# Re-cutting the transfers of a long-convolution and soft-MoE kernel to multiples of 16 rows

## The chip, the cores and the metric

The kernel runs on one core of a Trainium2 chip. The metric is device time in microseconds, taken as the median over several runs. A separate profiled execution gives the busy times, waits and transfers; its span is a little shorter than the timed runs, because it goes from the first to the last instruction.

## The reference

The input `x` is 8 sequences of 5696 tokens with 128 channels; `h` is one filter of 5696 taps for each channel. Each sequence is convolved with the filter along the tokens (a causal convolution, computed over a doubled length in the frequency domain). The 45568 result rows then go through a soft mixture of experts:

```python
Yf = rfft(x, n=2*S) * rfft(h, n=2*S);  y = irfft(Yf)[:, :S]      # 8 x 5696 x 128
logits = y.reshape(N, D) @ phi                                   # N = 45568, 32 slots
d = softmax(logits, over tokens);   slot_input = d.T @ y
slot_out[e] = relu(slot_input[e] @ w1[e]) @ w2[e]                # 8 experts x 4 slots
out = softmax(logits, over slots) @ slot_out
```

All data are float32.

## The kernel before

**Tiling.** The 5696 tokens of a sequence are laid out as 89 rows (`R1`) of 64 (`N2`). The transform is split into one over the rows (90 frequencies, `N1`, of which two halves of 45, `NP`) and one over the 64 columns. Everything is written as matrix products with constant tables: `s1` (rows to frequencies), `wt` and `vt` (columns, forward and back), and `i1` (frequencies back to rows).

**Stages.** The filter is group 0, the sequences are groups 1 to 8. A group is worked in 8 chunks of 4 columns and their mirror columns.

- Stage A: `load_x` (L190) brings a chunk of x or h into one of three `xc` tiles, as 80 rows at partition `X0` = 20 and 9 rows behind them. `fold` (POOL, L201) adds or subtracts the mirrored columns over all 128 partitions. `stage_a` multiplies by `s1` (PE, L212, two products per half), ACT copies the result from PSUM into `fst` (L214), and SyncE stores two blocks of 45 rows, from partitions `F0` = 6 and `F1` = 82, into the DRAM tensor `fd` (L218, f<-fst).
- Stage B: `load_g` (L236) brings 4 frequencies of `fd` back as a `gt` tile of 128 partitions, PE multiplies by `wt` (L250), DVE multiplies by the filter's spectrum (L268, L277), PE multiplies by `vt` (L292), ACT copies (L297), and SyncE stores the result into the DRAM tensor `zd` (L300, z<-zst).
- Stage C works on pairs of chunks, 32 in all: `load_pair` (L328, zc<-z) brings 90 rows of `zd`, 16 KB each, as 64 rows at partition 32 and 26 rows at partition 0. `stage_c1` multiplies by `i1` (L347) over all 128 partitions and builds the convolved rows `y`. The following stages transpose `y` (L375), form the logits (L384), the two softmaxes, and the weighted sum of rows per slot (`dispatch`, L460), one for each pair.
- At the end the experts are computed, and the output is formed and stored (L817, L828).

**Order.** Stages A, B and C of different groups are interleaved by a plan written out by hand: each step `t` does one chunk of A, one or two units of B, and half a pair of C. All large transfers are issued by SyncE in program order. Transfers take turns on eight completion counters, so a transfer waits for the one that stands eight places before it, besides the waits for its data.

**The edges of the blocks.** The products of L212 and L347 run over all 128 partitions, but x fills 89 of them and z 90. The rest must hold zeros: the `xc` tiles (L177) and the `zc` tile (L314) are cleared at the start. For the last pairs a second z tile, `zd`, is placed in memory that the front's tables have given up. There the rows from 26 to 31, between the two blocks, are copied from `zc` (L657), and L347 uses 96 partitions on that tile (`used`).

Of the kernel before, what the change touches and what calls it, by code (L numbers as in the profile page):

```python
# [10 lines left out]
F32 = mybir.dt.float32  # L11
# [5 lines left out]

def z_blocks(n):

    return [(0, 64, 32), (64, n - 64, 0)]  # L20


def transform_tables(S, N1, N2, CH, X0, F0, F1):

    N, R1, HALF, P = N1 * N2, S // N2, N2 // 2, 2 * N2
    k1 = np.arange(N1)
    alpha = np.pi * (k1 + 0.5) / N1
    m1 = np.arange(R1) - (N1 - 1) / 2
    a1 = np.outer(m1, alpha)  # L40
    s1 = np.stack([np.cos(a1), -np.sin(a1), -np.cos(a1)], 1)
    a0 = np.outer(alpha, np.arange(N1 // 2) + 0.5)
    i1 = np.stack([np.cos(a0), -np.sin(a0), -np.cos(a0)], 1)
    NP = N1 // 2
    part = s1
    s1 = np.zeros((P, 3, P))
    for a, p in enumerate((F0, F1)):
        s1[X0:X0 + R1, :, p:p + NP] = part[:, :, a * NP:(a + 1) * NP]
    part = i1[np.arange(N1).reshape(2, NP).T.reshape(-1)]
    i1 = np.zeros((P, 3, N2))  # L50
    for r, n, p in z_blocks(N1):
        i1[p:p + n, :, 0:NP] = part[r:r + n]
    k2 = np.arange(N2)
    omega = np.pi * (k1[:, None] + 2 * N1 * k2[None] + 0.5) / N
    m2 = np.arange(HALF) - (N2 - 1) / 2
    a2 = m2[None, :, None] * omega[:, None, :]
    w = np.concatenate([np.cos(a2), np.sin(a2)], 1)
    back = np.arange(N2).reshape(2, HALF // CH, CH).transpose(1, 0, 2).reshape(-1)
    NU = (NP + 1) // 2
    turn = (N1 - 1) / 2 * alpha[:, None] + (N2 - 1) / 2 * omega  # L60
    wq = np.zeros((2, N2, NP, N2))
    vq = np.zeros((2, N2, NU, 2, N2))
    tn = np.zeros((2, N2, 2, (NU + 1) // 2, 2, 2))
    for a in range(2):
        wq[a] = w[a * NP:(a + 1) * NP].transpose(1, 0, 2)
        for q in range(NP):
            vq[q % 2, :, q // 2, a] = w[a * NP + q][back].T
            tn[q % 2, :, 0, q // 4, a, q // 2 % 2] = np.cos(turn[a * NP + q]) / N
            tn[q % 2, :, 1, q // 4, a, q // 2 % 2] = np.sin(turn[a * NP + q]) / N
    wq, vq, tn = [t.reshape(P, *t.shape[2:]) for t in (wq, vq, tn)]  # L70
    return [np.ascontiguousarray(t, dtype=np.float32) for t in (s1, i1, wq, vq, tn)]
# [3 lines left out]
def kernel(  # L75
# [24 lines left out]
    nc = tc.nc  # L100
    P = 128
    B, S, D = x.shape
    NSL = moe_phi.shape[1]
    E, _, F = moe_w1.shape
    SPE = NSL // E
    NFC = F // P
    N1, N2 = 90, 64
    R1, HALF, NP = S // N2, N2 // 2, N1 // 2
    CH = 4
# [6 lines left out]
    HP = P // 2  # L116
    NQ = NJ // 2
    assert S == R1 * N2 and R1 == N1 - 1 and D == P and CH == Q == 4
    SPLIT = R1 // 16 * 16
    X0, F0, F1 = 20, 6, 82  # L120
    ctx.enter_context(tc.manual_schedule())

    t_s1, t_i1, t_w, t_v, t_turn = [
        nc.inline_tensor(t, f"tab_{n}").ap()
        for n, t in zip(("s1", "i1", "w", "v", "turn"), transform_tables(S, N1, N2, CH, X0, F0, F1))]
    fd = [nc.dram_tensor(f"f_{g}", (2, N2, NP, 2, D), F32, kind="Internal").ap() for g in range(B + 1)]
    zd = [nc.dram_tensor(f"z_{b}", (NP, 2 * N2, 2, D), F32, kind="Internal").ap() for b in range(B)]
    cd = nc.dram_tensor("c_t", (P, B * NQ, Q, 2, MH), F32, kind="Internal").ap()

# [6 lines left out]
    i1 = const.tile([P, 3, HP], F32, name="i1")  # L136
# [24 lines left out]
    s1 = apool.tile([P, 3, P], F32, name="s1", tag="s1", bufs=1)  # L161
    wt = fconst.tile([P, NP, HP], F32, name="wt")
    vt = fconst.tile([P, NU, 2, HP], F32, name="vt")
    turn = fconst.tile([P, 2, NW, 2, 2], F32, name="turn")
# [8 lines left out]
    xs = {}  # L173
    xf = [apool.tile([P, CH, D], F32, name=f"x{i}", tag=f"x{i}", bufs=1) for i in range(2)]
    xcs = [apool.tile([P, 2, CH, D], F32, name=f"xc{i}", tag=f"xc{i}", bufs=1) for i in range(3)]
    for t_ in xcs:
        nc.vector.memset(t_[:, :, :, :], 0.0)  # L177

    def load_x(c):
        if c >= (B + 1) * NJ:  # L180
            return
        g, j = divmod(c, NJ)
        src = (h if g == 0 else x[g - 1]).rearrange("(a n) d -> a n d", n=N2)
        t_ = xcs[c % len(xcs)]
        gap = N2 - CH * (2 * j + 1)
        for r in (slice(0, SPLIT), slice(SPLIT, R1)):
            v = src[r, CH * j:CH * (j + 1), :]
            v = bass.AP(tensor=v.tensor, offset=v.offset,
                        ap=[v.ap[0], [gap * D, 2], [1, CH * D]])
            nc.sync.dma_start(  # L190
                out=t_[X0 + r.start:X0 + r.stop, :, :, :].rearrange("p s n d -> p s (n d)"), in_=v)
        xs[c] = t_

    folded = {}
# [1 line left out]
    def fold(c, comp):  # L196
        if c not in xs:
            return
        t_ = xs.pop(c) if comp else xs[c]
        y_ = xf[comp]  # L200
        nc.gpsimd.tensor_tensor(out=y_[:, :, :], in0=t_[:, 0, :, :], in1=t_[:, 1, ::-1, :],  # L201
                                op=AL.subtract if comp else AL.add)
        folded[(c, comp)] = y_

    def stage_a(c, comp):
        g, j = divmod(c, NJ)
        src = folded.pop((c, comp))
        tab = (0, 1) if comp == 0 else (1, 2)
        st = apool.tile([P, CH, 2, D], F32, name="fst", tag="fst", bufs=5)
        for G in range(2):  # L210
            p = bank()
            nc.tensor.matmul(p[:, :], s1[:, tab[G], :],  # L212
                             src[:, :, :].rearrange("p n d -> p (n d)"), start=True, stop=True)
            nc.scalar.activation(st[:, :, G, :],  # L214
                                 p[:, :].rearrange("p (n d) -> p n d", d=D), AF.Copy)
        n0 = comp * HALF + CH * j
        for a, p in enumerate((F0, F1)):
            nc.sync.dma_start(  # L218
                out=fd[g][a, n0:n0 + CH, :, :, :].rearrange("n q c d -> q n (c d)"),
                in_=st[p:p + NP, :, :, :].rearrange("k n c d -> k n (c d)"))  # L220


    gs, prods = {}, {}
# [80 lines left out]


    zs, ys, Ls, ds = {}, {}, {}, {}
    zn = used = None
    ybufs = [ypool.tile([P, Q * CH, D + 1], F32, name=f"y{i}") for i in range(2)]
    zring = [ypool.tile([P, 2, 2, CH, 2, D], F32, name="zc")]
    lt = ypool.tile([P, CH, 2, HP], F32, name="lt")  # L310
    dt = ypool.tile([P, CH, 2, HP], F32, name="dt")
    om, op = [ypool.tile([P, CH, D], F32, name=n) for n in ("om", "op")]
    yt = ypool.tile([D, Q * CH, 2, MH], F32, name="yt")
    nc.vector.memset(zring[0][:, :, :, :, :, :], 0.0)  # L314
    for t_ in (lt, dt):
        nc.vector.memset(t_[:, :, :, :], 0.0)
    for t_ in ybufs:
# [15 lines left out]

    def stage_c1(T, between):
        t_ = zs.pop(T)
        kr = used if t_ is zn else P
        y_ = ybufs.pop(0)
        ybufs.append(y_)

        def part(v, f):  # L340
            k = (2 * v + f) * CH
            return y_[:, k:k + CH, 0:D] if f == 0 else y_[:, k + CH - 1:k - 1:-1, 0:D]

        def product(o, tab, q):
            p = bank()
            for h_ in range(2):
                nc.tensor.matmul(p[h_ * HP:(h_ + 1) * HP, :], i1[0:kr, tab, :],  # L347
                                 t_[0:kr, h_, o, :, q, :], start=True, stop=True)
            return p[:, :].rearrange("p (n d) -> p n d", d=D)

        def fold_out(even, minus, plus):
            nc.vector.tensor_tensor(out=plus, in0=even, in1=minus, op=AL.add)  # L352
            nc.vector.tensor_tensor(out=minus, in0=even, in1=minus, op=AL.subtract)

        b_, a_ = product(0, 1, 1), product(0, 0, 0)
        nc.scalar.activation(part(0, 0), b_, AF.Copy)
        fold_out(a_, part(0, 0), part(1, 0))
        between()
        b_, a_ = product(1, 1, 0), product(1, 2, 1)
        nc.scalar.activation(om[:, :, :], b_, AF.Copy)  # L360

        def after():
            fold_out(a_, om[:, :, :], op[:, :, :])
            for v, o_, eng in ((1, op, nc.gpsimd), (0, om, nc.vector if tail else nc.gpsimd)):
                for part_, sign in ((part(v, 1), AL.subtract), (part(v, 0), AL.add)):
                    eng.tensor_tensor(out=part_, in0=part(v, 0), in1=o_[:, :, :], op=sign)  # L366

        ys[T] = y_
        return after
# [191 lines left out]
    for t in range(last_front + 1):  # L561
# [82 lines left out]
        if NA < t <= NA + E:  # L644
# [2 lines left out]


    T = V + 1
    (_, n0, p0), (_, n1, p1) = z_blocks(N1)  # L650
    gap, used = slice(p1 + n1, p0), p0 + n0
    front.close()
    rings.append(mid.enter_context(tc.tile_pool(name="ps2", bufs=4, space=PSUM)))
    last = work.enter_context(tc.tile_pool(name="last", bufs=1))
    tail["last"] = last
    zn = last.tile([P, 2, 2, CH, 2, D], F32, name="zd")
    nc.sync.dma_start(out=zn[gap, :, :, :, :, :].rearrange("k h o n c d -> k (h o n c d)"),  # L657
                      in_=zring[0][gap, :, :, :, :, :].rearrange("k h o n c d -> k (h o n c d)"))
    zring.insert(0, zn)
    load_pair(V + 2)  # L660
    nc.sync.dma_start(out=w1s[:, E - 1, :], in_=moe_w1[E - 1])
# [4 lines left out]
    y_ = tail["pool"].tile([P, Q * CH, D + 1], F32, name="y2", tag="y2", bufs=1)  # L666
# [6 lines left out]
    for q in range(Q):  # L673
        r = slice(q * NSL, (q + 1) * NSL)
# [19 lines left out]
    for V in range(T, NT):  # L694
# [30 lines left out]
        else:  # L725
            for i in range(4 * (V - T - 1), min(4 * (V - T), E), 2):
                nc.sync.dma_start(
                    out=w2s[:, i:i + 2, :, :],
# [7 lines left out]
    p = bank()  # L736
# [127 lines left out]
```

## Time and profile before

| | before |
|---|---|
| time, median of 3 runs | 924.22 us (922.99 to 924.59) |
| span of the profiled execution | 914.5 us |
| granted TensorE clock, mean | 0.945 |
| bytes moved by transfers | 272.43 MB |
| L212 matmuls (stage A) | 576, 611 ns on average |
| L347 matmuls (stage C) | 512 |
| f<-fst stores | 288 of 180 KB |
| x and h loads | 72 of 320 KB and 72 of 36 KB |
| z loads | 32 of 1024 KB and 32 of 416 KB |

An engine's busy share is an average over stages with different limits. Three stretches matter here: the start, in which only stages A and then B run (to about 180 us), the middle in which all three stages run side by side (180 to 686 us), and the end. In a table of stretches each row gives its length, the busy time of each engine with the number of instructions, the granted clock, the mean busy share of the 16 DMA engines, and the rate of their traffic. The chain of waits runs back from the last instruction: a piece named DMA is time in which the work that ended last stood waiting for that transfer to land.

### The profile page before, as it was taken

The page shows a single profiled execution, that of the slowest core. Times are in us where ns is not written, and L with a number is a line of the kernel's source. Part 1 is how long each engine was busy: PE and PEld are TensorE (multiplying, and loading weights), DVE is VectorE, ACT ScalarE, POOL GpSimd, SP SyncE. Part 2 cuts the span into 40 slices and gives each one's busy share as a digit, 9 for nine tenths or more (in the row PEclk, how much of TensorE's full clock was granted, in tenths as well). Part 3 has the DMA queues.
Part 4 walks back from the last instruction along what each step waited for, and adds up shares of the span by engine and source line. Part 5 has one row for each costly group of instructions (what it writes and reads, how often), then busy time and mean ns, then how long its engine had stood idle before and what let it go on. Part 6 is the DMA issues. An engine that isn't in the chain of part 4 may idle for free.

```text
span 914.5 us, 19226 instructions
## 1 busy us (share of the span) xinstructions
PE 812.2 (89%) x7220; PEld 425.9 (47%) x7220; DVE 645.8 (71%) x928; ACT 481.1 (53%) x888; POOL 405.2 (44%) x385
## 2 busy tenths in 40 slices
PE   6968888799999999999999999999988776978893
PEld 2323344344454444544555445444444443345783
DVE  3058767667888878877888777868888885774552
ACT  4624445456556565655666565555654344474442
POOL 4624333245555555555555555555533432472000
PEclk9989999999999999999999999999999998788865
DMA  9999899999999999999999999989989998751798
GB/s 302 269 282 310 256 326 347 292 323 340 285 324 331 304 281 323 320 329 280 329 323 317 289 317 313 311 281 325 334 266 338 305 295 206 223 220 74 281 404 340
DMA packets 156550, 272.43 MB, mean 298 GB/s; under 512 B 11766, under 2 KB 114422, under 8 KB 153317
## 3 DMA queue, kind: packets, MB, share of 16 engines
q1 hardware_dynamic: 155883, 270.85, 91.7%
q8 instruction: 58, 0.95, 0.4%
q10 hardware_dynamic: 576, 0.36, 0.2%
q14 instruction: 33, 0.27, 0.1%
HBM read 142.86 MB, written 128.21 MB: 296 GB/s over the span
## 4 chain that ended last, share of the span: by engine, by line
PE 61%; DMA 27%; issue 4%; ACT 2%; DVE 2%; POOL 2%; SPq 1%; DVEq 0%; POOLq 0%; ACTq 0%
PE bank L212 19%; PE bank L347 10%; PE bt L250 9%; DMA zc<-z 8%; PE bz L292 7%; DMA gt<-f 6%; DMA out_dram<-o 4%; PE bank L375 3%; PE bank L460 3%; DMA zd<-z 3%; DMA z<-zst 2%; DMA f<-fst 2%; PE bank L384 2%; PE bank L436 2%; PE op L817 1%
## 5 line engine op out<-in xcount | busy, mean ns | idle before, releaser
L201 POOL TENSOR_TENSOR x<-xc 128x512 f32<-128x512 f32 x144 | 183.1, 1273 | 260.5 <-PE bank L212 156.9
L212 PE MATMUL bank<-x,s 128*128 128x512 f32 x576 | 273.9, 611 | 9.7 <-POOL x L201 9.6
L214 ACT ACTIVATE fst<-bank 128x512 f32<-128x512 f32 x288 | 171.8, 597 | 94.7 <-PE bank L212 88.3
L297 ACT ACTIVATE zst<-bz 128x1024 f32<-128x1024 f32 x96 | 93.2, 971 | 195.2 <-PE bz L292 191.5
L268 DVE TENSOR_TENSOR p<-bt,Hi 128x1024 f32<-128x1024 f32 x96 | 113.0, 1177 | 107.3 <-PE bt L250 107.1
L212 PEld LDWEIGHTS bank<-x,s 128*128 128x128 f32 x576 | 102.1, 192 | 126.9 <-issue 94.1
L250 PE MATMUL bt<-gt,wt 64*64 64x256 f32 x1620 | 117.4, 397 | 40.0 <-DMA gt<-f 19.8
L347 PE MATMUL bank<-zc,i 128*64 128x512 f32 x480 | 118.0, 614 | 8.5 <-DMA zc<-z 6.2
L277 DVE TENSOR_TENSOR yf<-bt,p 128x512 f32<-128x512 f32 x192 | 119.4, 663 | 3.3
L268 DVE TENSOR_TENSOR bt<-bt,Hr 128x1024 f32<-128x1024 f32 x96 | 113.0, 1178 | 0.0
L250 PEld LDWEIGHTS bt<-gt,wt 64*64 64x64 f32 x1620 | 55.9, 134 | 117.0 <-issue 61.7
L292 PE MATMUL bz<-yf,vt 64*64 64x256 f32 x1440 | 103.7, 386 | 0.0
L366 POOL TENSOR_TENSOR y<-y,op 128x512 f32<-128x512 f32 x64 | 77.4, 1209 | 11.8 <-DVE op L352 9.1
L292 PEld LDWEIGHTS bz<-yf,vt 64*64 64x64 f32 x1440 | 61.8, 136 | 21.1
L366 POOL TENSOR_TENSOR y<-y,om 128x512 f32<-128x512 f32 x54 | 64.0, 1185 | 2.1
L347 PEld LDWEIGHTS bank<-zc,i 128*64 128x64 f32 x480 | 30.9, 138 | 70.3 <-issue 47.4
L375 PE MATMUL bank<-ident,y 109*128 109x109 f32 x512 | 57.5, 268 | 0.7 <-DVE y L366 0.7
L375 PEld LDWEIGHTS bank<-ident,y 109*128 109x128 f32 x512 | 51.2, 146 | 12.9 <-POOL L L449 6.2
L421 POOL MEMSET dt<- 64x8 f32 x32 | 3.4, 106 | 115.9 <-issue 69.2
L377 ACT ACTIVATE yt<-bank 128x360 f32<-128x360 f32 x128 | 50.2, 483 | 2.1 <-PE bank L375 2.1
L817 PE MATMUL op<-so,cT 32*128 32x128 f32 x704 | 46.2, 369 | 4.3 <-ACT o L826 3.4
L268 DVE TENSOR_TENSOR p<-bt,turn 128x1024 f32<-128x1024 f32 (+1 forms) x12 | 14.1, 1176 | 50.7 <-PE bt L250 50.6
(97 smaller groups left out, 861.5 us busy)
## 6 DMA issues: line engine op xcount, KB each, us to landing
f<-fst SPq DMA_DIRECT2D x288, 180.0 KB
gt<-f SPq DMA_DIRECT2D x99, 512.0 KB
z<-zst SPq DMA_DIRECT2D x88, 512.0 KB
zc<-z SPq DMA_DIRECT2D x30, 1024.0 KB
xc<-in_x_dram SPq DMA_DIRECT2D x64, 320.0 KB
out_dram<-o SPq DMA_DIRECT2D x16, 1024.0 KB
zc<-z SPq DMA_DIRECT2D x30, 416.0 KB
out_dram<-o SPq DMA_DIRECT2D x8, 768.0 KB
```

The lines of the kernel that those rows point to most:

```text
L201: nc.gpsimd.tensor_tensor(out=y_[:, :, :], in0=t_[:, 0, :, :], in1=t_[:, 1, ::-1, :], op=AL.subtract if comp else AL.add)
L212: nc.tensor.matmul(p[:, :], s1[:, tab[G], :], src[:, :, :].rearrange("p n d -> p (n d)"), start=True, stop=True)
L214: nc.scalar.activation(st[:, :, G, :], p[:, :].rearrange("p (n d) -> p n d", d=D), AF.Copy)
L250: nc.tensor.matmul(bt[q * HP:(q + 1) * HP, a, o, :], wt[r, 2 * i + q, :], t_[r, 2 * o + q, :, :].rearrange("p c d -> p (c d)"), start=True ...
L268: nc.vector.tensor_tensor(out=p_, in0=pv, in1=h_, op=AL.mult)
L277: eng.tensor_tensor(out=y_[r, 0:k, c, :], in0=pv[:, :, c, :], in1=pi[r, 0:k, 1 - c, :], op=op_)
L292: nc.tensor.matmul(bz[a * HP:(a + 1) * HP, q, o, :], vt[r, i, a, :], y_[r, a * m + o, :, :].rearrange("p c d -> p (c d)"), start=True, sto ...
L297: nc.scalar.activation(st[:, 0:m, 0:n, :].rearrange("p o q x -> p q o x"), bz[:, 0:n, 0:m, :], AF.Copy)
L347: nc.tensor.matmul(p[h_ * HP:(h_ + 1) * HP, :], i1[0:kr, tab, :], t_[0:kr, h_, o, :, q, :], start=True, stop=True)
L366: eng.tensor_tensor(out=part_, in0=part(v, 0), in1=o_[:, :, :], op=sign)
L375: nc.tensor.transpose(p[:, i * TR:(i + 1) * TR], ys[T][0:TR, k * CH + i, 0:D], ident[0:TR, 0:TR])
L817: nc.tensor.matmul(pq[q][:, k * D:(k + 1) * D], cT[rows, b, r0:r0 + RW, :] if k < n else cL[rows, :, :], so4[rows, :], start=True, stop=True)
```

## The change

Each transfer that had another number of rows is cut into pieces of 16, 32, 48 or 64 rows.

- f: `fd` gets 48 frequencies for each half instead of 45 (`QR`); the three added rows are zero columns of `s1`. The stores take 48 partitions from `F0` = 8 and `F1` = 72.
- z: the second piece is 32 rows from row 58, six of which the first piece has already brought. In `i1` the repeated rows are zero. The two pieces fill partitions 0 to 95 without a gap.
- x: three pieces in place of two: 64 rows at partition 32, 16 rows at the even partitions 0 to 30, and 16 rows, seven of them repeated, at the odd partitions 1 to 31. In `s1` the repeated rows are zero.
- The fold and the products L212 and L347 run over 96 partitions (`KR`), all of which are now filled. So the clearing of `xc` and `zc`, the copy of the gap into `zd`, and `used` go.

The purpose is that every transfer has row counts that divide evenly over the 16 DMA engines, and that no cleared partitions are needed.

```diff
 def z_blocks(n):
-    return [(0, 64, 32), (64, n - 64, 0)]
+    return [(0, 64, 32), (n - 32, 32, 0)]
+def x_blocks(n):
+    return [(0, 64, 32, 1), (64, 16, 0, 2), (n - 16, 16, 1, 2)]
...
-    SPLIT = R1 // 16 * 16
-    X0, F0, F1 = 20, 6, 82
+    F0, F1 = 8, 72
+    QR = 48
+    KR = 96
...
-    fd = [nc.dram_tensor(f"f_{g}", (2, N2, NP, 2, D), F32, kind="Internal").ap() for g in range(B + 1)]
+    fd = [nc.dram_tensor(f"f_{g}", (2, N2, QR, 2, D), F32, kind="Internal").ap() for g in range(B + 1)]
...
-    for t_ in xcs:
-        nc.vector.memset(t_[:, :, :, :], 0.0)
...
-        for r in (slice(0, SPLIT), slice(SPLIT, R1)):
-            v = src[r, CH * j:CH * (j + 1), :]
+        for r, n, p, step in x_blocks(R1):
+            v = src[r:r + n, CH * j:CH * (j + 1), :]
...
-                out=t_[X0 + r.start:X0 + r.stop, :, :, :].rearrange("p s n d -> p s (n d)"), in_=v)
+                out=t_[p:p + (n - 1) * step + 1:step, :, :, :].rearrange("p s n d -> p s (n d)"), in_=v)
...
-        nc.gpsimd.tensor_tensor(out=y_[:, :, :], in0=t_[:, 0, :, :], in1=t_[:, 1, ::-1, :],
+        nc.gpsimd.tensor_tensor(out=y_[0:KR, :, :], in0=t_[0:KR, 0, :, :], in1=t_[0:KR, 1, ::-1, :],
...
-            nc.tensor.matmul(p[:, :], s1[:, tab[G], :],
-                             src[:, :, :].rearrange("p n d -> p (n d)"), start=True, stop=True)
+            nc.tensor.matmul(p[:, :], s1[0:KR, tab[G], :],
+                             src[0:KR, :, :].rearrange("p n d -> p (n d)"), start=True, stop=True)
...
-                in_=st[p:p + NP, :, :, :].rearrange("k n c d -> k n (c d)"))
+                in_=st[p:p + QR, :, :, :].rearrange("k n c d -> k n (c d)"))
...
-    nc.vector.memset(zring[0][:, :, :, :, :, :], 0.0)
...
-                nc.tensor.matmul(p[h_ * HP:(h_ + 1) * HP, :], i1[0:kr, tab, :],
-                                 t_[0:kr, h_, o, :, q, :], start=True, stop=True)
+                nc.tensor.matmul(p[h_ * HP:(h_ + 1) * HP, :], i1[0:KR, tab, :],
+                                 t_[0:KR, h_, o, :, q, :], start=True, stop=True)
...
-    nc.sync.dma_start(out=zn[gap, :, :, :, :, :].rearrange("k h o n c d -> k (h o n c d)"),
-                      in_=zring[0][gap, :, :, :, :, :].rearrange("k h o n c d -> k (h o n c d)"))
```

More of the change, by code (lines that the diff above doesn't have):

```diff
@@ L18, in z_blocks, with transform_tables @@
 def z_blocks(n):
-    return [(0, 64, 32), (64, n - 64, 0)]
-def transform_tables(S, N1, N2, CH, X0, F0, F1):
+    return [(0, 64, 32), (n - 32, 32, 0)]
+def x_blocks(n):
+    return [(0, 64, 32, 1), (64, 16, 0, 2), (n - 16, 16, 1, 2)]
+def transform_tables(S, N1, N2, CH, F0, F1):
     N, R1, HALF, P = N1 * N2, S // N2, N2 // 2, 2 * N2
@@ L47, in transform_tables @@
     for a, p in enumerate((F0, F1)):
-        s1[X0:X0 + R1, :, p:p + NP] = part[:, :, a * NP:(a + 1) * NP]
+        done = 0
+        for r, n, p0, step in x_blocks(R1):
+            for i in range(n):
+                if r + i >= done:
+                    s1[p0 + i * step, :, p:p + NP] = part[r + i, :, a * NP:(a + 1) * NP]
+            done = max(done, r + n)
     part = i1[np.arange(N1).reshape(2, NP).T.reshape(-1)]
     i1 = np.zeros((P, 3, N2))
+    done = 0
     for r, n, p in z_blocks(N1):
-        i1[p:p + n, :, 0:NP] = part[r:r + n]
+        i1[p + done - r if r < done else p:p + n, :, 0:NP] = part[max(r, done):r + n]
+        done = r + n
     k2 = np.arange(N2)
@@ L124 @@
         nc.inline_tensor(t, f"tab_{n}").ap()
-        for n, t in zip(("s1", "i1", "w", "v", "turn"), transform_tables(S, N1, N2, CH, X0, F0, F1))]
-    fd = [nc.dram_tensor(f"f_{g}", (2, N2, NP, 2, D), F32, kind="Internal").ap() for g in range(B + 1)]
+        for n, t in zip(("s1", "i1", "w", "v", "turn"), transform_tables(S, N1, N2, CH, F0, F1))]
+    fd = [nc.dram_tensor(f"f_{g}", (2, N2, QR, 2, D), F32, kind="Internal").ap() for g in range(B + 1)]
     zd = [nc.dram_tensor(f"z_{b}", (NP, 2 * N2, 2, D), F32, kind="Internal").ap() for b in range(B)]
@@ L306 @@
     zs, ys, Ls, ds = {}, {}, {}, {}
-    zn = used = None
+    zn = None
     ybufs = [ypool.tile([P, Q * CH, D + 1], F32, name=f"y{i}") for i in range(2)]
@@ L335, in stage_c1 @@
         t_ = zs.pop(T)
-        kr = used if t_ is zn else P
         y_ = ybufs.pop(0)
@@ L649 @@
     T = V + 1
-    (_, n0, p0), (_, n1, p1) = z_blocks(N1)
-    gap, used = slice(p1 + n1, p0), p0 + n0
     front.close()
```

## The prediction

> **What bounds the kernel now.** I read the page first (busy shares, packet counts, chain of waits), then the stretch table, then the chain in order of time, then the matmul groups with shapes kept apart.
>
> ```profile
> PE 812.2 (89%) x7220; PEld 425.9 (47%) x7220; DVE 645.8 (71%) x928; ACT 481.1 (53%) x888; POOL 405.2 (44%) x385
> DMA packets 156550, 272.43 MB, mean 298 GB/s; under 512 B 11766, under 2 KB 114422, under 8 KB 153317
> q1 hardware_dynamic: 155883, 270.85, 91.7%
> PE 61%; DMA 27%; issue 4%; ACT 2%; DVE 2%; POOL 2%; SPq 1%; DVEq 0%; POOLq 0%; ACTq 0%
> ...
> xc<-in_x_dram SPq DMA_DIRECT2D x64, 320.0 KB
> ...
> zc<-z SPq DMA_DIRECT2D x30, 416.0 KB
> ```
>
> TensorE holds most of the chain, but transfers hold 27% of it; the last two lines are two of the transfers that the change re-cuts (320 KB are 80 rows, 416 KB are 26). The stretch table (length, then busy time of PE, PEld, DVE, ACT, POOL, granted clock, DMA share, GB/s) splits that up:
>
> ```profile
> 46.00:114.00 68.00, 53.49 (x304) 22.38 (x304) 48.58 (x56) 23.68 (x40) 24.38 (x20) 0.92 0.92 283
> 180.00:686.00 506.00, 491.81 (x4352) 246.50 (x4354) 400.26 (x575) 297.90 (x543) 267.74 (x249) 1.00 0.98 311
> 760.00:835.00 75.00, 56.84 (x455) 30.69 (x455) 47.09 (x83) 42.27 (x100) 38.60 (x46) 0.81 0.68 206
> ```
>
> In the long middle, PE is busy 97% and the 16 DMA engines 98%: both are nearly full. From 46 to 114 us PE is idle for 14.5 us with the DMA at 92%. The chain shows where the middle loses time:
>
> ```profile
> 213.89 1.02 PE bank L460 x32
> ...
> 235.13 1.03 PE bank L460 x32
> ...
> 298.23 12.96 DMA zc<-z
> 311.33 1.94 PE bank L347 x8
> ...
> 651.30 1.02 PE bank L460 x32
> ```
>
> A pair of steps (one L460 to the next) takes 20.7 to 21.2 us where PE flows; from 213.89 to 651.30 there are 20 pairs, so 21.87 us on average. The difference, about 0.7 us a pair, is a handful of stalls on zc<-z and gt<-f loads that stand deep in a full queue.
>
> [...] the counter writes are f 4320, gt 1728, z 1536, zc 928, x 1800 and 1198 for the rest, 64 for the four ACT-issued constants, and 256 short rows of phi and turn: 11766 in all, as the page has. [...] from 180 to 686 us the 2 KB packets of x took 127 ns on average against a floor of 82, the 16 KB packets of z 835 against 611 [...], while 88% of the 128-partition gt packets are near their floor. [...] 94% of the 1 KB packets sit at 46 ns[...]. [...] here the 64 KB pitch of z still gives 611 ns per 16 KB, so a pitch of 48 KB for f instead of 45 KB is costed at nothing.
>
> **The change part by part.** *Engines per transfer.* [...] Worth by itself: 0. [...]
>
> *Where the x rows land.* [...] That is the ratio of the z load [...], whose mean is 1.37 of its floor, against 1.55 for x now. I take 115 ns a packet: 12 packets x 12 ns = 0.14 us a load [...]. Bounds: 127 ns (nothing) and 82 ns (0.54 us). There are 38 such loads in the middle: 5.5 us (0 to 20, but PE, busy 492 of 506, caps it near 12). Some ten more from 46 to 114 us: 1.5 us. These are on the path as far as the engines' queue sets the pair's time.
>
> *SyncE's queue.* 72 more x issues at 0.4 to 0.5 us (median 394 ns for h, 520 for x): 36 us of SP time, 2 per pair. Behind them stand the f stores and the gt load of the same step. SP is idle some 7 us in a pair, waiting on engines, so I cost it at 0 to 1 us in all while the queue is full. The eight completion counters are handed out in turn, so each transfer waits for the one eight places before. In before, gt mostly waits for the 64-row z load; in after for the 32-row one, which lands a little later, and the fourth f store waits for the 64-row one. Behind gt is the z store, and PE L250 waits for gt (27.5 us in all). The queue ahead of gt holds the same transfers either way, and 3 to 5 us of work is still in flight: I take +1.5 us in total, bounds 0 and +10.
>
> *96 partitions.* The trace has the same matmul on 96 rows, in the last pairs (before, too, skips the zero rows there):
>
> ```profile
> L347 PE MATMUL bank<-zc,i x480: 592/593/1116, 181.6 to 810.4; 128*64 128x512 f32 x160
> L347 PE MATMUL bank<-zd,i x32: 592/1061/1116, 775.6 to 800.4; 96*64 96x512 f32 x32
> ```
>
> Minimum, and the slow-clock figure, are the same (592, 1116), so 576 matmuls of L212 and 480 of L347 gain nothing. The POOL fold (1273 ns) keeps its 512 elements per partition: 0.
>
> *Start and end.* The xc memsets (first one 1.02 to 1.93 us, on the path of the first load) go: -1.2 us, +0.5 for the third x issue: -0.7. The zc memset (3.5 us) was beside the first transfers: 0. The 6-row copy into zd (0.80 us of SP at 759.85) went ahead of the zd load for which PE waits: -0.8.
>
> Sum: -5.5 - 1.5 + 1.5 - 0.7 - 0.8 = -7; I take 1 off for stalls that don't shrink with the load: -6, so 918.
>
> **Rivals.** *Unchanged (924):* [...] if the x packets stay at 127 ns, the start and end gains (1.5) meet the wait for the later z load. [...] *PE alone becomes the bound (908):* x packets fall to 85 to 95 ns, the DMA stalls vanish; 20 of the middle's 24 pairs' 0.7 us, so -13, and -3 elsewhere. For it: pairs of 20.7 us occur. Against: zc loads keep their size [...]. *Slower through the queue (931):* 23 instead of 21 transfers per pair among eight counters means fewer bytes in flight; each zc load holds gt back by 0.3 to 0.4 us more, 24 times, +7 to +8. For it: SP already waits 51.8 us at L236 for zc and 40.1 for f. Against: the share of 0.98. *Slower through bytes (945):* if the packets above their floor come from a limit shared by all engines, 3.2% more bytes cost up to 3.2% of 700 us, +22. Against: the slices of the page reach 404 GB/s in the output stage, well above the 311 here.
>
> **How the numbers follow.** Forecast (around 918) 0.45, PE bound 0.12, unchanged 0.16, queue 0.20, bytes 0.07. The bound of 0.2% is 1.85 us: faster 0.57, same 0.15, slower 0.28. The range takes in the PE-bound case and the queue case: 907 to 933.
>
> **What would show it.** Right: under 512 B the packets become 11766 + 288 + 96 + 1656 - 6 = 13800; DMA share in the middle near 1.00, with some 325 GB/s there; pairs of 21.5 us; L212 and L347 at 592 ns; POOL's wait for xc below 85.8 us. Wrong: an unchanged or longer wait of PE L250 for gt and of L347 for zc, or SP waits at L236 and at the fourth f store grown by over 10 us (queue); store packets slower than 46 ns (bytes); PE idle gone from the middle (PE bound).

## The result, and the profile after

The changed kernel takes 991.67 us against 924.4 us before: the ratio is 1.071 (95% interval 1.065 to 1.077), so it is 7.1% slower, and outside the range given. Ratios here and below compare only the executions within 1.5% of each kernel's fastest, while medians are over all of them. The page of the changed kernel, in the parts shown of before (busy time, packets, the chain by engine):

```profile
PE 844.8 (85%) x7220; PEld 439.2 (44%) x7220; DVE 632.6 (64%) x924; ACT 481.1 (49%) x888; POOL 404.9 (41%) x385
DMA packets 163171, 281.09 MB, mean 284 GB/s; under 512 B 13800, under 2 KB 119912, under 8 KB 159752
q1 hardware_dynamic: 162504, 279.51, 90.6%
PE 44%; DMA 41%; issue 4%; ACT 3%; SPq 3%; DVE 3%; POOL 1%; DVEq 0%; ACTq 0%; POOLq 0%
```

The number of tiny packets is the 13800 that was worked out. On how many engines a transfer runs was not shown: the packet records do not name the engine. The rate fell from 298 to 284 GB/s with 3% more bytes to move, and transfers hold 41% of the chain instead of 27%. The table of stretches:

```profile
46.00:114.00 68.00, 52.03 (x255) 21.05 (x255) 39.64 (x44) 21.49 (x36) 23.65 (x19) 0.87 0.88 264
180.00:686.00 506.00, 458.54 (x3836) 229.33 (x3836) 346.81 (x503) 265.63 (x481) 240.06 (x221) 0.96 0.97 290
```

In the same 506 us PE gets through 3836 matmuls instead of 4352, at 290 GB/s instead of 311, though the DMA share is still 0.97. From the starts of the L460 groups in the two traces: the first group begins at 242.9 us instead of 213.8, the next 20 pairs take 484.5 us instead of 437.4 (24.2 us each instead of 21.9), and the rest 263.7 instead of 263.2. So 29 us are lost in the start, 47 in the middle, nothing at the end. (The traces are 77 us apart and the medians 67: the profiled execution of before took 916.4 us, less than its median, so its span is short for that reason too.) PE itself is not slower per instruction at full clock; 96 rows take the same 592 ns (shapes kept apart, nanoseconds as minimum/median/maximum):

```profile
L223 PE MATMUL bank<-x,s x576: 591/592/1222, 7.2 to 746.8; 96*128 96x512 f32 x192
L356 PE MATMUL bank<-zc,i x480: 592/592/1117, 203.7 to 883.0; 96*64 96x512 f32 x160
```

SyncE's own waits for zc in the middle (who waited for what: us in total, times, longest) have moved. In before it was gt (L236) and behind it the z store (L300) that waited; now it is an f store (L229), and gt (L247) waits a second time behind it. Before, then changed:

```profile
SPq L236 <- DMA zc<-z: 51.8, 15, 4.7
SPq L300 <- DMA zc<-z: 24.6, 17, 2.3
```

```profile
SPq L229 <- DMA zc<-z: 53.8, 17, 4.8
SPq L247 <- DMA zc<-z: 25.4, 15, 2.5
```

Their sum hardly differs (81.5 us in before with two small lines more, 79.2 after). What differs is the place: the wait comes one transfer earlier, with the last f store and gt still to be issued. Over the whole kernel PE's wait for gt grew from 27.5 to 48.9 us and its wait at L347 for zc from 6.2 to 23.2.

### The profile page after: what moved, and what is told of

Read it like the earlier page. It is cut to its first block, busy times and chain, and to the rows that moved or that the text cites. A ratio compares the mean times of both kernels' runs of the same rounds, so it can differ in the third digit from the quotient of the medians.

```text
span 991.1 us, 19314 instructions
## 1 busy us (share of the span) xinstructions
PE 844.8 (85%) x7220; PEld 439.2 (44%) x7220; DVE 632.6 (64%) x924; ACT 481.1 (49%) x888; POOL 404.9 (41%) x385
## 2 busy tenths in 40 slices
DMA packets 163171, 281.09 MB, mean 284 GB/s; under 512 B 13800, under 2 KB 119912, under 8 KB 159752
## 4 chain that ended last, share of the span: by engine, by line
PE 44%; DMA 41%; issue 4%; ACT 3%; SPq 3%; DVE 3%; POOL 1%; DVEq 0%; ACTq 0%; POOLq 0%
DMA zc<-z 19%; PE bank L223 13%; DMA gt<-f 10%; PE bank L356 10%; PE bt L261 7%; PE bz L303 4%; DMA out_dram<-o 3%; DMA z<-zst 3%; DMA xc<-in_x_dram 2%; PE bank L469 2%; PE bank L445 2%; DMA f<-fst 1%; PE op L822 1%; PE bank L422 1%; PE bank L384 1%
## 5 line engine op out<-in xcount | busy, mean ns | idle before, releaser
L212 POOL TENSOR_TENSOR x<-xc 96x512 f32<-96x512 f32 x144 | 182.5, 1269 | 331.1 <-PE bank L223 197.4
L223 PE MATMUL bank<-x,s 96*128 96x512 f32 x576 | 286.3, 634 | 12.8 <-POOL x L212 12.8
L261 PE MATMUL bt<-gt,wt 64*64 64x256 f32 x1620 | 121.8, 409 | 60.7 <-DMA gt<-f 38.7
L223 PEld LDWEIGHTS bank<-x,s 96*128 96x128 f32 x576 | 106.7, 200 | 138.7 <-issue 103.0
L356 PE MATMUL bank<-zc,i 96*64 96x512 f32 x480 | 130.6, 669 | 32.3 <-DMA zc<-z 23.2
L261 PEld LDWEIGHTS bt<-gt,wt 64*64 64x64 f32 x1620 | 59.0, 138 | 141.1 <-issue 71.4
L303 PE MATMUL bz<-yf,vt 64*64 64x256 f32 x1440 | 107.0, 391 | 0.0
L356 PEld LDWEIGHTS bank<-zc,i 96*64 96x64 f32 x480 | 33.7, 147 | 99.0 <-issue 66.9
L303 PEld LDWEIGHTS bz<-yf,vt 64*64 64x64 f32 x1440 | 64.7, 138 | 20.7 <-issue 1.9
```

The costliest lines, as they stand in the source:

```text
L212: nc.gpsimd.tensor_tensor(out=y_[0:KR, :, :], in0=t_[0:KR, 0, :, :], in1=t_[0:KR, 1, ::-1, :], op=AL.subtract if comp else AL.add)
L223: nc.tensor.matmul(p[:, :], s1[0:KR, tab[G], :], src[0:KR, :, :].rearrange("p n d -> p (n d)"), start=True, stop=True)
L261: nc.tensor.matmul(bt[q * HP:(q + 1) * HP, a, o, :], wt[r, 2 * i + q, :], t_[r, 2 * o + q, :, :].rearrange("p c d -> p (c d)"), start=True ...
L303: nc.tensor.matmul(bz[a * HP:(a + 1) * HP, q, o, :], vt[r, i, a, :], y_[r, a * m + o, :, :].rearrange("p c d -> p (c d)"), start=True, sto ...
L356: nc.tensor.matmul(p[h_ * HP:(h_ + 1) * HP, :], i1[0:KR, tab, :], t_[0:KR, h_, o, :, q, :], start=True, stop=True)
```

## The experiments

Ratios are to the kernel before, with 95% intervals. Theories: *pitch* (48 KB rows of f), *sixteenth engine* or *filled engines* (the added bytes slow all), *count* (the third x transfer), *z ports* (the z load with the longer second piece is slower); later *counters* (which transfer waits for which) and *issue* (SyncE's time per transfer).

### Each part alone

The edits are shown in short form, here and below.

```diff
-    fd = [nc.dram_tensor(f"f_{g}", (2, N2, NP, 2, D), ...
+    fd = [nc.dram_tensor(f"f_{g}", (2, N2, 48, 2, D), ...           # f_pitch48, f_rows48
...
-                in_=st[p:p + NP, :, :, :] ...
+                in_=st[p:p + 48, :, :, :] ...                       # f_rows48 alone, with F0, F1 = 8, 72
...
-        for r in (slice(0, SPLIT), slice(SPLIT, R1)):
+        for r, n, p, step in x_blocks():                            # x_three: 64, 16, 16 rows
...
-    return [(0, 64, 32), (64, n - 64, 0)]
+    return [(0, 64, 32), (n - 32, 32, 0)]                           # z_32: and no copy of the gap
```

> The kernel before with one edit: the DRAM tensor of f has room for 48 frequencies per half, so its row pitch is 48 KB instead of 45 KB; the stores still take 45 rows, no byte and no transfer is added. Theory 'pitch' (reads and writes at 48 KB steps are slower): 15 to 45 us slower than before, with gt packets slower. Theories 'sixteenth engine' [...], 'count' (the third x transfer) and 'z ports' [...]: within 3 us of before.

> The kernel before with the f part alone: pitch 48 KB and stores of 48 rows from partitions 8 and 72, [...] (+3.5 MB). Theory 'sixteenth engine': 20 to 45 us slower, and slower than the run with the pitch alone. Theory 'pitch': the same as the run with the pitch alone. 'Count' and 'z ports': within 3 us of before.

> The kernel before with the x part alone: three transfers (64, 16, 16 rows) in place of two (80, 9); memsets and 128-partition products stay. Theory 'count' (72 more transfers among eight counters, fewer bytes in flight): 20 to 60 us slower, DMA share in the middle lower than 0.98. 'Sixteenth engine': 5 to 12 us slower (2.1 of 8.6 MB). 'Pitch' and 'z ports': within 3 us, or up to 8 us faster [...].

> The kernel before with the z part alone: the second z piece is 32 rows instead of 26 (six repeated), and the copy of the gap rows goes. Theory 'z ports': 15 to 40 us slower, z packets slower than 835 ns. 'Sixteenth engine': 8 to 20 us slower (3.1 of 8.6 MB). 'Pitch' and 'count': within 3 us.

| run | us | ratio |
|---|---|---|
| f_pitch48 | 927.5 | 1.002 (0.999 to 1.005) |
| f_rows48 | 933.1 | 1.009 (1.005 to 1.012) |
| z_32 | 923.4 | 0.997 (0.994 to 1.000) |
| x_three | 971.2 | 1.053 (1.043 to 1.062) |

The pitch costs nothing that can be measured, the 48 rows under 1%, the z part nothing. The x part alone brings most of the loss, as *count* said, and in both places: its first dispatch (L460 in before) comes 15 us later than in before, its 20 pairs take 33 us longer.

### What in the x part

Two things set it apart besides its rows. It adds a third transfer, and SyncE needs longer to issue each of its pieces. SyncE's issue times for x and h loads, before (80 and 9 rows) and changed (64 rows, and 16 rows at a partition step of 2):

```profile
L190 SPq DMA_DIRECT2D xc<-in_x_dram x128: 282/520/1462, 33.3 to 642.3; - x128
L190 SPq DMA_DIRECT2D xc<-in_h_dram x16: 312/394/864, 2.0 to 30.2; - x16
```

```profile
L201 SPq DMA_DIRECT2D xc<-in_x_dram x192: 569/619/1992, 39.9 to 719.3; - x192
L201 SPq DMA_DIRECT2D xc<-in_h_dram x24: 577/600/1276, 0.7 to 36.6; - x24
```

The least time of an x load doubles, from 282 to 569 ns. The expectations call an issue with the shorter time the short issue path. Four kernels take the two things apart.

```diff
+    nc.dge_precook = False                                         # x_slow: round the x loads only
-    for r in (slice(0, SPLIT), slice(SPLIT, R1)):
+    for r in (slice(0, 48), slice(48, SPLIT), slice(SPLIT, R1)):   # x_split
+    return [(0, 80, 16, 1), (73, 16, 0, 1)]                        # x_two16
+    for r in (slice(0, 96),) if 0 < g < B else (...)               # x_one: X0 = 0
```

> The kernel before with its own two x transfers (80 and 9 rows, same rows, partitions, bytes and number), but taken off the short issue path: the build's mark for it is cleared on the 144 x loads alone. Theory 'issue' (SyncE needs some 600 ns instead of 320 to 400 for each such transfer, and what stands behind it in the queue comes late): 10 to 30 us slower than before, with x issues at 570 ns or more. Theory 'count' (one more transfer per step among eight counters): within 3 us of before. Theory 'placement' (partitions and rows of the three pieces): within 3 us.

> The kernel before with three x transfers (48, 32 and 9 rows) on the same partitions and with the same bytes; all three keep the short issue path. Theory 'count': 35 to 50 us slower, as the run with the x part alone. Theory 'issue': 8 to 25 us slower (one more issue of 0.35 to 0.5 us for each load, against 1.0 us for the x part). 'Placement': within 3 us.

> The kernel before with x as two transfers of 80 rows at partition 16 and 16 rows (seven repeated) at partition 0: row counts in multiples of 16, [...] the same number of transfers, the short issue path. Theories 'issue' and 'count': within 5 us of before. Theory 'sixteen rows' (the added rows and filled engines themselves cost): 10 us or more slower.

> The kernel before with one x transfer of 96 rows from partition 0 for the first seven sequences; the seven rows beyond the 89 belong to the next sequence and meet zeros in s1. The filter and the last sequence keep 80 and 9 rows. One issue and one counter less for each of 56 loads. Theories 'issue' and 'count': 5 to 20 us faster than before. 'Sixteen rows' (added bytes cost): 3 to 10 us slower.

| run | us | ratio |
|---|---|---|
| x_slow | 934.6 | 1.009 (1.006 to 1.013) |
| x_split | 959.4 | 1.039 (1.031 to 1.046) |
| x_two16 | 941.8 | 1.018 (1.012 to 1.025) |
| x_one | 923.1 | 0.998 (0.995 to 1.001) |

In x_slow the loads are the same 80 and 9 rows, issued with the setting in the first line of the edits off, and the least time doubles there too, from 282 to 591 ns:

```profile
L191 SPq DMA_DIRECT2D xc<-in_x_dram x128: 591/823/1550, 37.2 to 659.8; - x128
```

SyncE's issue durations add up to 457.9 us in before, 503.4 in x_slow and 503.2 in x_split. Both add 45 us (the three loads of x_split keep a least time of 292 ns), but x_slow costs 9 us and x_split 35, with the same bytes to the same partitions. So SyncE's time is the small part, and the third place in the turn of the eight counters the large one. x_one moves more bytes than before (317 GB/s in the middle) and loses nothing; it gains nothing either, where 5 to 20 us were expected, although the wait for z falls on the z store there (L300, 40.3 us) and hardly on gt. x_two16 is a miss: the same number of transfers as before, a least issue time of 321 ns, and yet 1.8%. Its rows lie elsewhere, 16 of them on partitions 0 to 15, and its 2 KB packets take 138 ns instead of 127, and it moves 2.1 MB more; which of these costs it was not tried.

### Who waits for the z load

In the turn of eight, the transfer that stands eight places behind the 64-row z load waits until that load has landed. With two x transfers this is the gt load. Behind the first of the two z loads stand the second, two of x and four of f; SyncE is done with these at 304.21 us and issues gt, the eighth, only at 308.95 (SyncE's order in before: start and length in us):

```profile
297.59 2.09 SPq L328 DMA_DIRECT2D zc<-z  x2
299.78 1.36 SPq L190 DMA_DIRECT2D xc<-in_x_dram  x2
301.23 2.98 SPq L218 DMA_DIRECT2D f<-fst  x4
308.95 0.34 SPq L236 DMA_DIRECT2D gt<-f  x1
```

With three it is the fourth f store, and gt is then caught by the second z piece. SyncE's waits in the middle, x_split:

```profile
SPq L218 <- DMA zc<-z: 73.3, 18, 6.2
...
SPq L236 <- DMA zc<-z: 21.5, 16, 2.4
```

PE in turn waits longer for gt (whole kernel; before, then x_split):

```profile
PE bt L250 <- DMA gt<-f: 19.8, 13, 6.9
```

```profile
PE bt L250 <- DMA gt<-f: 33.3, 21, 8.3
```

The next kernels leave the transfers as they are and are meant to change only this.

```diff
+        if t < NA:
+            load_x(t + 3)          # x_split_swap, after_swap, before_swap: ahead of the z load
         if pair(-2) is not None:
             load_pair(pair(-2))
-        if t < NA:
-            load_x(t + 3)
...
+    (nc.gpsimd if r.start == SPLIT else nc.sync).dma_start(        # x_split_pool
```

> The three-piece x load of the run before (48, 32, 9 rows), with one more edit: in each step the x load is issued before the z load instead of after it. The transfers, their sizes and the issue time stay; only who stands eight places behind the slow z load changes: the next step's x load in place of this step's fourth f store. Theory 'counters' (SyncE stands at the fourth f store until the z load has landed, and the engines run dry): recovers at least 15 of the 35 us, about 935 to 945, with the wait of the f store for zc (73 us) gone. Theory 'issue' (SyncE's time per issue): unchanged, 955 to 965.

> The changed kernel with the same exchange of the x load and the z load in the order of issue. 'Counters': recovers 25 us or more of the 67, 940 to 965. 'Issue' and 'filled engines' (8.6 MB more [...]): unchanged, 985 to 995.

> The three-piece x load with the 9-row piece issued by GpSimd, which has counters of its own: SyncE issues two x transfers and the eight counters turn as in the kernel before, while the engines still see three transfers. 'Counters' and 'issue': back near before, 920 to 933. If three smaller transfers themselves are what costs on the engines: 950 to 960.

> The kernel before with only the x load issued ahead of the z load. 'Counters': gt no longer waits for the z load (51.8 us of SyncE's waits), so 900 to 922; if z itself then comes too late, by the 356 KB that now stand ahead of it: 925 to 940.

| run | us | ratio |
|---|---|---|
| x_split_swap | 939.5 | 1.012 (1.003 to 1.020) |
| after_swap | 964.8 | 1.043 (1.034 to 1.052) |
| x_split_pool | 938.9 | 1.012 (1.005 to 1.018) |
| before_swap | 920.7 | 0.988 (0.983 to 0.993) |

Exchanging two calls takes 20 of the 35 us back as the medians stand, and by the ratios, each against before in its own round, 2.7 of 3.9% (some 25 us); of the changed kernel's 67 us it takes 27 back. *Issue* said nothing would change. The f store's wait for zc is gone. The new wait falls on the next step's x load, which three buffers cover, or, in a step that has one, on the c_t store (L495) (waits of SyncE, then of PE, x_split_swap):

```profile
SPq L495 <- DMA zc<-z: 34.0, 13, 4.6
...
SPq L190 <- DMA zc<-z: 19.9, 18, 3.8
...
SPq L218 <- DMA zc<-z: 1.7, 1, 1.7
```

```profile
PE bt L250 <- DMA gt<-f: 20.9, 13, 7.5
```

The middle follows (stretch table, x_split and then x_split_swap): 4060 matmuls become 4269, 295 GB/s become 308.

```profile
180.00:686.00 506.00, 470.39 (x4060) 235.93 (x4062) 371.11 (x534) 281.80 (x511) 253.08 (x234) 0.99 0.97 295
```

```profile
180.00:686.00 506.00, 484.57 (x4269) 242.08 (x4261) 391.65 (x558) 292.62 (x531) 264.00 (x244) 1.00 0.98 308
```

The exchange alone would not be a clean test. It also brings x earlier (POOL's wait for x falls from 94.9 to 10.3 us) and changes what is under way at once: x packets take 103 ns instead of 139, z packets 926 instead of 854. In x_split_pool these stay at 80.3 us, 137 and 855 ns. There the third piece takes no place on SyncE or in its turn, and gt waits for z as in before:

```profile
SPq L236 <- DMA zc<-z: 58.5, 16, 5.2
```

It lands at the same time, between the two values that had been expected. So some 25 us of the third transfer come from the turn, by two ways. Some 11 us stay in both, and what they are is open; part may lie in the start, where the first L460 comes at 222.0 us (x_split_swap) and 226.3 (x_split_pool), against 213.8 in before and 218.2 in f_pitch48.

In before the exchange is not settled. Gt's wait for z goes, but PE waits longer for z itself (21.2 us at L347 instead of 6.2). The ratio is 0.988; over all 12 executions, which spread from 907.6 to 930.7 us, the mean is only 0.5% below that of before (0.995, about 0.990 to 0.999).

### Do full engines cost?

```diff
+    X0, F0, F1 = 20, 8, 72                                         # f_and_z: the edits of f_rows48 and z_32
+        for r in (slice(0, 96),) if 0 < g < B else (...)           # f_z_x_one: f_and_z, with x as in x_one
+    return [(0, 48, 48, 1), (48, 32, 16, 1), (n - 16, 16, 0, 1)]   # after_swap_short: after_swap, other x_blocks
```

> The changed kernel without its x part: f stores of 48 rows and z pieces of 64 and 32 rows, but x as before (80 and 9 rows), with the memsets. If x carries the loss: 925 to 937 (the two parts alone gave +0.9% and -0.3%). If the parts only hurt together ('filled engines': 6.6 of the 8.6 MB): 950 to 980.

> All three parts with every row count a multiple of 16 (f 48, z 64 and 32, x one transfer of 96 rows where the rows exist): as many bytes [...] as the changed kernel, but one x transfer in place of three. 'Counters and issue': 922 to 938. 'Filled engines': 970 to 995.

> The changed kernel with the order exchanged, and with the three x pieces cut as 48, 32 and 16 rows at unit partition steps (still 96 rows, multiples of 16[...]), so that all three keep the short issue path. 'Issue' carries what the exchange left (965 against the 938 of the three short pieces): 935 to 950. If the remainder is full engines and bytes[...]: 958 to 975.

f_and_z takes 934.7 us, 1.011 (1.008 to 1.013); f_z_x_one 936.2, 1.011 (1.002 to 1.019). In the second nearly all row counts are multiples of 16, and 1% is what this costs with one x transfer; whether it fills more engines was not shown. The parts add up: x_three's 5.3% and f_and_z's 1.1% make 6.4 of the 7.1%, within the intervals. after_swap_short, 958.3 us, 1.037 (1.030 to 1.044), can't be told from after_swap, though SyncE's issue durations fall from 577 to 502 us: the longer issue is not most of what the exchange left. (Its pieces also land elsewhere.) f and z (1.1%) and the rest of the third transfer (1.2%) make 2.3 of the 3.7%; the remainder is open. The start at least is not repaired: the first dispatch comes at 244 us there, against 243 in the changed kernel, and for most of the start no z load is in the queue. One candidate was not taken apart. The changed kernel and its two variants, the only ones with products over 96 partitions throughout, were granted a mean PE clock of 0.90 to 0.93 in every execution, x_three 0.94. But x_one_z48, without such products, had 0.92 to 0.93 too, and what the clock costs was not measured.

### Beating both

```diff
+    return [(0, 48, 48), (n - 48, 48, 0)]      # z_blocks, with x as in x_one: x_one_z48
+    return [(0, 64, 32), (n - 32, 32, 0)]      # z_blocks, with x as in x_one: x_one_z32; best_swap: and the exchange
```

> An attempt to beat both kernels: x as one transfer of 96 rows where the rows exist (one issue and one counter less), and z as two transfers of 48 rows (six repeated), [...] without the copy of the gap. f as in before. 'Counters' and 'issue': 905 to 920. If the middle is already held by TensorE (492 of 506 us busy): 918 to 924. 'Filled engines': 925 to 932.

> An attempt to beat both kernels: the single x transfer with the z pieces of 64 rows at partition 32 and 32 rows at partition 0 (each alone gave 0.2 to 0.3% less). If the small gains add: 916 to 921. If TensorE already holds the middle: 921 to 926.

> The single x transfer, the z pieces of 64 and 32 rows, and the x load issued ahead of the z load. The exchange alone gave -1.2%, the single x and the z piece together -0.3%. If they add: 908 to 916. If they take the same wait away: 912 to 920. If TensorE holds the middle: 918 to 924.

| run | us | ratio |
|---|---|---|
| x_one_z48 | 996.8 | 1.076 (1.068 to 1.083) |
| x_one_z32 | 921.2 | 0.997 (0.994 to 0.999) |
| best_swap | 911.2 | 0.984 (0.978 to 0.990) |

best_swap is the fastest of all: one x transfer, z as 64 and 32 rows, x issued ahead of z. x_one_z48 is the surprise. Against x_one only the cut of z differs (and the copy of the gap is gone), and it loses 74 us. The middle of x_one, then of x_one_z48:

```profile
180.00:686.00 506.00, 494.46 (x4396) 248.29 (x4396) 409.21 (x582) 301.59 (x549) 270.84 (x252) 1.00 0.99 317
```

```profile
180.00:686.00 506.00, 454.34 (x3854) 224.58 (x3854) 352.74 (x509) 267.98 (x487) 244.31 (x226) 0.97 1.01 288
```

Here the engines are the busiest of all and yet move less (a share of 1.01 means that more than 16 packets are in flight in the records on average). A 16 KB packet of z takes about 1260 ns on average instead of 840, and a tenth of them are near the floor instead of over half.

## Why the prediction was wrong

**The step that failed is SyncE's queue**: "I take +1.5 us in total, bounds 0 and +10". The prediction saw that the fourth f store would wait for the 64-row z load and gt for the 32-row one. It then argued that the queue holds the same transfers either way, and 3 to 5 us of work. x_split measured that term by itself: +35 us (3.9%) for the third transfer, of which the exchange returns some 25.

Why the work in flight was not enough can be read from the packet records. With 14 packets or fewer in flight, at least two of the 16 engines have none. That holds for 0.14 of the middle in before, 0.18 in x_split, 0.20 in x_three and 0.19 in the changed kernel. While SyncE waits at the f store, the engines are still fed (0.05 of x_split's 73 us). In the 3 us after each such wait they are not: 0.46 of this time in x_split, 0.39 in x_three and 0.23 in the changed kernel (0.47 there after gt's second wait), against 0.16 after gt's wait for z in before and 0.10 after the x load's in x_split_swap. So what stands behind the wait is issued too late. This measure does not carry all of it: after_swap has 0.20 of the middle, although 27 us came back.

**The slower rival was the right kind, and its size wrong.** "Each zc load holds gt back by 0.3 to 0.4 us more, 24 times, +7 to +8" priced the delay of the landing alone. The signs that it named came true: SyncE's waits for zc at gt and the f stores grew from 54 to 79 us, PE's for gt and for zc as above. But a pair lost 2.4 us, and the start, which has no z load for most of its length (in before the first is issued at 170 us), lost 29 us, which no rival foresaw. Of these x_split shows 13 and x_three 15, x_slow and f_pitch48 under 5; but x_two16 and f_z_x_one, without a third transfer, show 10 and 11. Each is a single profiled execution, and what costs in the start stays open.

**The issue time was taken from the old shapes.** 72 more x issues at 0.4 to 0.5 us, 36 us in all, did not hold: all 216 took 569 ns or more, and SyncE's issue durations grew from 458 to 575 us. x_slow puts a rise of 45 us at 0.9%.

**The x gain did not come.** The 115 ns a packet were an estimate of the author from the z load, whose packets took 1.37 of their floor; x_three shows 125 and the changed kernel 130, against 127. The new cut of x paid nothing. The exchange did shorten the packets, with the same rows in the same places (130 ns to 95 from the changed kernel to after_swap): what was under way beside them counted for more.

**Two zeros were nearly right.** 48 rows of f cost 0.9% and were priced at 0; the z part came out at 0.997. That the added bytes by themselves cost little did hold: f_z_x_one, with nearly all row counts multiples of 16, is 1.1% slower (1.019 at most) and not the 2.4% of the "bytes" rival's 22 us, so that rival falls.

**One sum was loose.** In the count of tiny packets the 1198 "for the rest" already hold the 64 of the constants; only so do the terms make 11766.

**Right:** the 13800 tiny packets, matmuls of 96 rows at 592 ns, the pitch at nothing. The gains at the two ends, 1.5 us, are too small to be seen here.

## What to carry to other kernels

Where transfers share a turn of completion counters, one more transfer in a step changes which one waits for the slowest load (before, SyncE stood 51.8 us for it at gt; in x_split, 73.3 us at the f store); list, for each transfer, the one that stands as many places before it as there are counters, and place a patient one there. That paid clearly where the third transfer had put an f store there, and not clearly in before. A free exchange in the order of issue was worth more here than any recut of the rows (0.984 for best_swap against 0.997 for x_one_z32). Row counts in multiples of 16 gained nothing by themselves here (1.011 for f_and_z and for f_z_x_one), and splitting a load has a price in issue time that must be taken from the new shape (569 ns or more a piece here, against 282 or more before).

## What the runs showed of the hardware

- How long SyncE takes to issue a load depends on more than its bytes. The least time for x loads of 80 and 9 rows is 282 ns, and 591 for the same loads with one setting of the build off (x_slow); for the loads of 64 rows, and of 16 with a partition step of 2, it is 569 in the changed kernel and in x_three.
- How long a packet takes depends on what is under way beside it. From x_split to x_split_swap, where only the order of issue differs, the 2 KB packets of x fall from 139 to 103 ns and the 16 KB packets of z rise from 854 to 926.
- How a load is cut, and where its rows land, can cost as much as the whole change: z in two pieces of 48 rows instead of 64 and 32, with the same bytes, takes 997 us against 921 (x_one_z48, x_one_z32). Its 16 KB packets of z take about 1260 ns on average, against 840 in before with 64 and 26 rows. Why was not tried.
- PE's mean granted clock was 0.945 before and 0.916 after, so part of PE's longer busy time (845 against 812 us) is the lower clock. Stalls alone do not bring it down: x_three, with 461 us of PE work in the 506 us of the middle (459 after), was granted 0.944. The cause is open.
